# The last unit of a tiled matrix product: a bank of its own for one product, and another queue for two stores

## The chip, the cores and the metric

The kernel runs on one core of one Trainium2 chip. The metric is the device time of one execution in microseconds (us). A core has TensorE (PE, matrix products), VectorE (DVE), ScalarE (ACT), GpSimd (POOL) and SyncE (SP). Each works through its own list of instructions in order. DMA transfers are issued from the lists of SP and ACT here; the issuing instruction takes its place in that list, and the transfer itself is carried out by DMA engines. Matrix products are written into PSUM[...]; VectorE and ScalarE read them there.

## The reference

```
attention: q, k, v of (4, 8, 768, 64); each query sees only the keys that
           have the same nearest centroid (16 per head); softmax; times v
x        = the result as (3072, 512)
h        = x @ w_in            # (3072, 2048)
g        = relu(h) ** 2
out      = g @ w_out           # (3072, 512)
```

The change concerns the last part of the last batch, a piece of `g @ w_out`.

## The kernel before

The kernel first does the attention of all heads, with the rounding of the weights beside it. Then it takes the four batches in the order `FEED`, one after the other (n = 0 to 3). For each it computes `g` in `up` (or `first_up`) and then the product with `w_out` in `Down.run` (or `first_down` for n = 0). Both use a scheme that makes a product of two-by-two blocks from seven block products and a number of sums; in `Down` it is used twice, one level inside the other.

`Down.run` goes through `self.units`. A unit is a pair `(of, j)`: `j` is one of the seven products of the outer level, and `of` says which set of rows it is for. For the last batch there are 14 units, the last being `(1, 3)`. Within one unit the inner level makes seven products. `times` makes each with four matmuls that add up in PSUM. Their results go to two banks, `one` and `two`: `one[:, 0]`, `one[:, 1]`, `one[:, 2]` and `two[:, 0]` to `two[:, 3]`, 128 columns each. The order on TensorE is `one[:, 0]`, `two[:, 0]`, `two[:, 1]`, `two[:, 2]`, `two[:, 3]`, `one[:, 2]`, `one[:, 1]`. So `two[:, 3]` is the fourth product of the bank `two`, and `one[:, 1]` the seventh of the unit.

ScalarE copies `one[:, 0]` to the tile `copied`; behind this copy, in ScalarE's list, `self.store()` issues the stores that are noted in `self.stores`. VectorE puts the seven products together in the generator `combine`, which runs one unit later than the products it uses, in two halves. The first half is three adds on `two` into `r`: one of 256 columns on the first two blocks, one of 128 on the third, one of 256 on the fourth. The second half adds `r` to the result tile `c[...]` (512 columns), and adds `one[:, 1:3]` (256 columns). When a result is complete, `combine` notes it in `self.stores`, and `store` sends it out one unit later as two transfers of 128 KB, by `store_block` (L1104), from ScalarE's list.

For the last unit there is nothing to run behind it, and its combining is a little different. The seventh product goes to a bank of its own, `last`. `one[:, 2]` and `last` are added apart, 128 columns each, and each half of the result is stored as soon as it is ready: the half with the sixth from SP's list, the other from ScalarE's. After the loop, `list(waiting)` runs this last combining, and `self.store()` then issues what is still noted: the result `(0, 12)` of the unit in front, which was combined while the last unit's products ran.

The order on each engine is that of the program (`manual_schedule`). Banks come from the pool `banks` of six, in rotation, by `bank_tile`. A wait is set where an instruction reads a tile that another engine writes, and it is for the whole of what has been written into that tile's bank so far in program order.

At the very end all engines load a flag (L1263) and branch (L1276) over a general path that other inputs would need. SP then waits for all transfers to be complete, and the engines meet in a closing barrier (L1460).

Of the kernel before, what the change touches and what calls it, by code (L numbers as in the profile page):

```python
# [18 lines left out]
P = 128  # L19
# [6 lines left out]
def kernel(  # L26
# [10 lines left out]
    nc = tc.nc  # L37

    B, H, S, D = q.shape
# [510 lines left out]
    def sub(out, a, b, eng=nc.vector):  # L550
        return eng.tensor_tensor(out=out, in0=a, in1=b, op=ALU.subtract)  # L551
# [61 lines left out]
    for p in range(NG):  # L613
# [37 lines left out]
        first, last = total[p][:, :, 0:QA], total[p][:, :, QA:S]  # L651
# [71 lines left out]
    def bank_tile(width):  # L723
        return banks.tile([P, width], F32, name="bank", tag="bank")
# [8 lines left out]
    def combine(c, product, width, early=(), behind_copy=None, behind_add=None):  # L733
        (c11, c12), (c21, c22) = c
        waiting = {}

        def bank_of(j):
            if j in waiting:
                return waiting[j]
            bank = bank_tile(width)  # L740
            product(j, bank)
            return bank

        def add(j, *results):
            bank = bank_of(j)
            for out, to in results:
                nc.vector.tensor_tensor(out=out, in0=bank, in1=to, op=ALU.add)  # L747
            if behind_add:
                behind_add(j)

        bank = bank_tile(width)
        product(1, bank)
        nc.scalar.copy(out=c11, in_=bank)
        if behind_copy:
            behind_copy()
        for j in early:
            waiting[j] = bank_of(j)
        add(6, (c12, c11))
        add(2, (c11, c11))
        add(7, (c21, c12))  # L760
        add(5, (c22, c21), (c12, c12))
        sub(c21, c21, bank_of(4))
        add(3, (c12, c12))
# [91 lines left out]
    def plus(out, one, two):  # L855
        nc.vector.tensor_tensor(out=out, in0=one, in1=two, op=ALU.add)
# [42 lines left out]
    def right(j):  # L899
        return {1: w_q[0][0], 2: w_q[1][0], 3: w_q[1][1], 4: w_t.get(4), 5: w_t.get(1),  # L900
                6: w_t.get(2), 7: w_t.get(3)}[j]
# [16 lines left out]
    def slot(k):  # L918
        first = F2 * PAIR + (k % 2) * F4 * P
        return home[k // 2 * 2][:, first : first + F4 * P].rearrange("p (f n) -> p f n", f=F4)  # L920

    def quarters(y):
        return [[y[:, F4 * g : F4 * (g + 1), P * m : P * (m + 1)] for m in range(2)] for g in range(2)]
# [12 lines left out]
    def load_right(j):  # L936
        for k in (1, 2, 0, 3):
            nc.sync.dma_start(slot(k), w_far[j - 1, k].rearrange("p (f n) -> p f n", f=F4))
# [15 lines left out]
    def first_level(g, f):  # L954
        a = block_of(g, f, TWO)
        s1, s2 = (s_home(i)[:, f] for i in range(2))
        plus(s1, a[1][0], a[1][1])
        sub(s2, s1, a[0][0])
        sub(a[1][0], a[0][0], a[1][0])

    def store_third(g, n, f):
        nc.sync.dma_start(g_far[n][f, :, 1:3], g[:, F2 + f, :, THIRD])
        if n % 2 == 0:
            nc.sync.dma_start(g_far[n][f, :, 0], g[:, f, 0, THIRD])
# [12 lines left out]
    def times(bank, left, rhs):  # L977
        for f in range(F4):
            nc.tensor.matmul(  # L979
                bank, lhsT=left[:, f], rhs=rhs[:, f], start=(f == 0), stop=(f == F4 - 1)  # L980
            )
# [6 lines left out]
    class Down:  # L988
# [77 lines left out]
                c[12] = tile(outp, "osb")  # L1066


        def combine(self, of, j, one, two, copied, last=None):
            c = self.c[of]  # L1070
            r = c[{1: 11, 4: 21, 5: 12, 7: 22}[j]] if j in (1, 4, 5, 7) else four_r
            plus(r[:, 0:2], two[:, 0:2], copied.unsqueeze(1).to_broadcast([P, 2, P]))
            plus(r[:, 2], two[:, 2], r[:, 1])
            plus(r[:, 1:4:2], two[:, 3].unsqueeze(1).to_broadcast([P, 2, P]), r[:, 1:3])
            yield
            if j in (2, 3):
                to = c[{2: 11, 3: 12}[j]]
                plus(to, to, r)
                if last is None:
                    plus(to[:, 1:3], one[:, 1:3], to[:, 1:3])  # L1080
                else:
                    plus(to[:, 2], one[:, 2], to[:, 2])
                    self.store_block(of, 12, 1, nc.sync)
                    plus(to[:, 1], last, to[:, 1])
                    self.store_block(of, 12, 0, nc.scalar)
                    return
            else:
                plus(r[:, 1:3], one[:, 1:3], r[:, 1:3])
            if j == 7:
                sub(c[21], c[22], c[21])  # L1090
            elif j == 6:
                plus(r, c[11], r)
                for to in (21, 12):
                    plus(c[to], c[to], r)
                plus(c[22], c[22], c[12])
            for to in {6: (21, 22), 2: (11,), 3: (12,)}.get(j, ()):
                self.stores.append((of, to))
# [8 lines left out]
                self.c[of][to][:, 2 * i : 2 * i + 2],  # L1106
            )

        def store(self):
            for of, to in self.stores:  # L1110
                for i in range(2):
                    self.store_block(of, to, i, nc.scalar)
            self.stores = []

        def run(self):
            first_level(self.g, F2 - 1)
            store_third(self.g, self.n, F2 - 1)
            waiting = None
            for u, (of, j) in enumerate(self.units):
                x, s = self.ahead  # L1120
                y = quarters(right(j))
                copied = spare_tile[:, 4 + u % 2]
                one, two = (
                    bank_tile(4 * P).rearrange("p (i n) -> p i n", i=4) for _ in range(2)
                )
                times(one[:, 0], x[0][0], y[0][0])
                nc.scalar.copy(out=copied, in_=one[:, 0])  # L1127
                self.store()
                times(two[:, 0], x[0][1], y[1][0])
                times(two[:, 1], s[:, 1], slot(1))  # L1130
                times(two[:, 2], x[1][0], slot(2))
                times(two[:, 3], s[:, 0], slot(0))
                times(one[:, 2], x[1][1], slot(3))
                if waiting:
                    next(waiting)
                sub(x[0][1], x[0][1], s[:, 1])
                last = None
                if self.n == B - 1 and u + 1 == len(self.units):
                    last = bank_tile(P)
                times(one[:, 1] if last is None else last, x[0][1], y[1][1])  # L1140
                if u + 1 < len(self.units):
                    if (k := self.units[u + 1][1]) != j:
                        load_right(k)
                    if of and j in LATER:
                        self.load_left(LATER[j])
                    if self.units[u - 1] == (0, 5):
                        sub(self.s1, self.a[0][1], self.s2)
                    self.parts()
                if u == 0:
                    store = third_sums(self.g, self.n, F2 - 1)  # L1150
                    self.find_results()
                    if self.n % 2:
                        self.load_left(4)
                        self.load_left(1)
                    store()
                    if self.n % 2:
                        self.load_left(5)
                if waiting:
                    next(waiting, None)
                waiting = self.combine(of, j, one, two, copied, last)  # L1160
                to_end = len(self.units) - 1 - u
                for kk in LOADS[self.n % 2].get(u, ()):
                    load_x(self.n + 1, kk)
                if to_end == 2 - self.n % 2:
                    sum_x(self.n + 1, 1)
                elif to_end == 0:
                    sum_x(self.n + 1, 2)
            list(waiting)
            sum_x(self.n + 1, 1)
            self.store()  # L1170
# [71 lines left out]
    def load_x(n, kk):  # L1242
        if n < B:
            b = FEED[n]
            if b not in xT:
                xT[b] = xp.tile([P, KT, S], F32, name="xT", tag="x1")
            nc.sync.dma_start(xT[b][:, kk], x_far[b][:, kk])
# [3 lines left out]
    def sum_x(n, steps):  # L1251
        if n < B:
            if n not in x_summed:
                x_summed[n] = [x_sums(FEED[n])]
            for _ in range(steps):
                x_summed[n].append(next(x_summed[n][0]))
# [208 lines left out]
```

## Time and profile before

| What | Value |
|---|---|
| time, median of 3 runs | 886.84 us (885.61 to 886.95) |
| profiled execution, its own time | 885.83 us |
| its span, first to last instruction | 884.0 us (884.04 in the trace's own record) |
| granted TensorE clock, mean | 0.998 |
| PE busy | 876.0 us, 99% of the span |
| DVE busy | 702.7 us, 79% |
| ACT busy | 390.2 us, 44% |
| from 872.00 to 878.40 us: PE, DVE, ACT busy | 5.48, 4.04, 0.27 us |
| from 878.40 us to the end: PE, DVE, ACT busy | 0, 0, 0 us |
| DMA share from 878.40 us to the end | 0.32 |

The profile is of one execution; its time is 1.8 us longer than the span, and the instructions lie in the span. A span of an engine's list that isn't counted as busy (issue of DMAs, branches, waits) can still be read: such rows have the engine's name with a q, as ACTq. The page's chain of waits is empty for this trace. In the timeline a row with x8 for PE is one product of four matmuls, each recorded twice.

### The profile page before, as it was taken

The numbers are of one execution on the slowest core, as the hardware profiler recorded it, in microseconds if no ns is written. First come the engines' busy times: TensorE is split into PE (matmuls) and PEld (weight loads), VectorE is DVE, ScalarE is ACT, GpSimd is POOL, SyncE is SP. The second block draws the span as 40 slices with busy tenths as digits, with TensorE's granted clock in tenths as the row PEclk, the third lists the DMA queues.
The fourth block names the chain that finished last, engine by engine and source line by source line (L and its number), as shares of the span: only waits on it lengthen the run. The fifth ranks groups of instructions, "written<-read, shape, count | busy, mean of one in ns | idle before, by whom it ended". The sixth has DMA issues, their size and how long they took to land.

```text
span 884.0 us, 14579 instructions
## 1 busy us (share of the span) xinstructions
PE 876.0 (99%) x5379; PEld 584.3 (66%) x5379; DVE 702.7 (79%) x1272; ACT 390.2 (44%) x621; POOL 145.5 (16%) x168
## 2 busy tenths in 40 slices
PE   9999999999999999999999999999999999999997
PEld 5444444444444455568855589996557975569996
DVE  6799888888888999999756586796568786576785
ACT  5877667777666657740045510003543024530000
POOL 0000000000010247730132200013320042300000
PEclk9999999999999999999999999999999999999999
DMA  6777787767763335236811156583113751118563
GB/s 251 177 189 193 218 263 186 201 179 211 212 161 101 102 134 171 72 121 225 309 36 49 42 166 194 155 268 105 51 51 105 237 162 37 52 60 247 153 196 115
DMA packets 166401, 136.04 MB, mean 154 GB/s; under 512 B 58826, under 2 KB 140082, under 8 KB 166066
## 3 DMA queue, kind: packets, MB, share of 16 engines
q1 hardware_dynamic: 149650, 119.65, 45.3%
q10 hardware_dynamic: 16672, 15.37, 5.7%
q8 instruction: 45, 0.74, 0.3%
q14 instruction: 34, 0.28, 0.1%
HBM read 82.10 MB, written 41.89 MB: 140 GB/s over the span
## 4 chain that ended last, share of the span: by engine, by line


## 5 line engine op out<-in xcount | busy, mean ns | idle before, releaser
L457 ACT ACTIVATE ex<-sc 128x1024 f32<-128x1024 f32 x144 | 144.3, 1026 | 37.5 <-PE sc L441 32.5
L747 DVE TENSOR_TENSOR g<-bank,g 128x384 f32<-128x384 f32 x192 | 102.5, 552 | 73.2 <-PE bank L790 67.8
L441 PE MATMUL sc<-qkT 64*128 64x512 f32 (+1 forms) x768 | 150.5, 484 | 0.0
L766 ACT ACTIVATE g<-g 128x384 f32<-128x384 f32 x122 | 63.4, 520 | 104.4 <-DVE g L747 100.2
L441 PEld LDWEIGHTS sc<-qkT 64*128 64x128 f32 x768 | 65.7, 188 | 42.1 <-issue 30.2
L790 PE MATMUL bank<-xT,w_in 128*128 128x384 f32 x256 | 93.2, 487 | 0.0
L790 PE MATMUL bank<-xT,w_s 128*128 128x384 f32 x256 | 93.1, 486 | 0.0
L1127 ACT COPY spare<-bank 128x128 f32<-128x128 f32 x35 | 9.3, 264 | 189.9 <-PE bank L979 165.9
L790 PE MATMUL bank<-x_t,w_s 128*128 128x384 f32 x256 | 93.0, 486 | 0.0
L475 PE MATMUL av_a<-ex,v_raw 128*64 128x512 f32 x384 | 85.9, 596 | 0.0
L460 DVE TENSOR_TENSOR total<-total,ex 128x1024 f32<-128x1024 f32 x64 | 78.7, 1229 | 6.5
L571 POOL TENSOR_TENSOR w_s<-w_in 128x256 f32<-128x256 f32 x32 | 25.2, 787 | 315.9 <-PE bank L979 148.4
L979 PE MATMUL bank<-home,l 128*128 128x128 f32 x560 | 74.0, 275 | 0.0
L790 PEld LDWEIGHTS bank<-xT,w_s 128*128 128x128 f32 x256 | 48.6, 190 | 34.2 <-issue 0.6
L790 PEld LDWEIGHTS bank<-x_t,w_s 128*128 128x128 f32 x256 | 48.6, 190 | 33.9
L790 PEld LDWEIGHTS bank<-xT,w_in 128*128 128x128 f32 x256 | 48.3, 190 | 33.7 <-DVE g L551 0.6
L161 POOL TENSOR_TENSOR w_in<-w_in,w_raw 128x512 int32<-128x512 int32 x16 | 21.4, 1337 | 294.3 <-DVE w_in L153 294.3
L979 PEld LDWEIGHTS bank<-home,l 128*128 128x128 f32 x560 | 68.2, 192 | 0.1
L767 ACT ACTIVATE g<-g 128x384 f32<-128x384 f32 x122 | 63.8, 523 | 3.9
L475 PEld LDWEIGHTS av_a<-ex,v_raw 128*64 128x64 f32 x384 | 26.1, 137 | 51.0 <-issue 50.3
L450 PE MATMUL sc<-rows 64*128 64x512 bf16 (+1 forms) x360 | 58.8, 323 | 0.0
L790 PE MATMUL bank<-x_t,w_in 128*128 128x384 f32 x128 | 46.5, 486 | 0.0
(192 smaller groups left out, 1408.6 us busy)
## 6 DMA issues: line engine op xcount, KB each, us to landing
home<-w_far SPq DMA_DIRECT2D x92, 256.0 KB
words<-flat SPq DMA_DIRECT2D x26, 384.0 KB
w_raw<-in_moe_w_in_dram SPq DMA_DIRECT2D x16, 512.0 KB
w_raw<-in_moe_w_out_dram SPq DMA_DIRECT2D x16, 512.0 KB
w_far<-home SPq DMA_DIRECT2D x28, 256.0 KB
g<-g_far SPq DMA_DIRECT2D x28, 256.0 KB
v_raw<-in_v_dram SPq DMA_DIRECT2D x16, 384.0 KB
g_far<-third SPq DMA_DIRECT2D x24, 256.0 KB
```

The source lines that it names most:

```text
L161: nc.gpsimd.tensor_tensor(out=dst, in0=dst, in1=lo, op=ALU.add)
L441: nc.tensor.matmul(sc[i][:, e, cols], lhsT=qkT[pair][rows, NCH + c], rhs=qkT[pair][rows, n.start // P : n.stop // P], start=first, stop=no ...
L450: nc.tensor.matmul(sc[i][:, e, cols], lhsT=ohT[pair][rows, 1, c * P : (c + 1) * P], rhs=ohT[pair][rows, 0, columns(i)], start=first, stop= ...
L457: nc.scalar.activation(out=ex[i], in_=sc.pop(i), func=ACT.Exp, scale=SCALE)
L460: eng.tensor_tensor(out=out, in0=a, in1=b, op=ALU.add)
L475: nc.tensor.matmul(bank[D * e : D * (e + 1), 0 : n.stop - n.start], lhsT=raw_v[pair][:, e, c], rhs=ex[i][:, e, cols], start=c == 0, stop=c ...
L571: nc.gpsimd.tensor_tensor(out=s1, in0=a[1][0], in1=a[1][1], op=ALU.add)
L747: nc.vector.tensor_tensor(out=out, in0=bank, in1=to, op=ALU.add)
L766: nc.scalar.activation(out=to, in_=to, func=ACT.Relu)
L767: nc.scalar.square(to, to)
L790: nc.tensor.matmul(bank, lhsT=operands[j][0][:, kk], rhs=operands[j][1][:, kk], start=(kk == 0), stop=(kk == H2 - 1),)
L979: nc.tensor.matmul(bank, lhsT=left[:, f], rhs=rhs[:, f], start=(f == 0), stop=(f == F4 - 1))
```

## The change

In the last unit of the last batch, the block product that was `two[:, 3]` is written to a new bank `five` (128 columns). `combine` reads `five` in its third add. In all other units `five` is `two[:, 3]`, as before. The bank `last` is taken at the unit's start with `five`.

The result `(0, 12)`, two transfers of 128 KB, is issued from SP's list instead of ScalarE's, and before the last combining in program order. So SP's list ends with these two stores and the store of the last result's first half; ScalarE's list ends with one store, that of the other half, where it ended with three.

```diff
-        def combine(self, of, j, one, two, copied, last=None):
+        def combine(self, of, j, one, two, five, copied, last):
...
-            plus(r[:, 1:4:2], two[:, 3].unsqueeze(1).to_broadcast([P, 2, P]), r[:, 1:3])
+            plus(r[:, 1:4:2], five.unsqueeze(1).to_broadcast([P, 2, P]), r[:, 1:3])
...
-        def store(self):
+        def store(self, queue=nc.scalar):
             for of, to in self.stores:
                 for i in range(2):
-                    self.store_block(of, to, i, nc.scalar)
+                    self.store_block(of, to, i, queue)
...
+                ends = self.n == B - 1 and u + 1 == len(self.units)
+                five = bank_tile(P) if ends else two[:, 3]
+                last = bank_tile(P) if ends else None
...
-                times(two[:, 3], s[:, 0], slot(0))
+                times(five, s[:, 0], slot(0))
...
-                last = None
-                if self.n == B - 1 and u + 1 == len(self.units):
-                    last = bank_tile(P)
-                times(one[:, 1] if last is None else last, x[0][1], y[1][1])
+                times(last if ends else one[:, 1], x[0][1], y[1][1])
...
-                waiting = self.combine(of, j, one, two, copied, last)
+                waiting = self.combine(of, j, one, two, five, copied, last)
...
+            if self.n == B - 1:
+                self.store(nc.sync)
             list(waiting)
             sum_x(self.n + 1, 1)
             self.store()
```

## The prediction

> **What bounds the kernel now.** The page's first part says that TensorE is never free:
>
> ```profile
> PE 876.0 (99%) x5379; PEld 584.3 (66%) x5379; DVE 702.7 (79%) x1272; ACT 390.2 (44%) x621; POOL 145.5 (16%) x168
> ```
>
> The change takes no matmul away and adds none, so it can only act where TensorE is done: behind the last product. The chain of waits on the page is empty for this trace, so I followed the end by hand. First the timeline of the last 10 us (start, length, engine, line, operation):
>
> ```profile
> 874.38 0.42 DVE L856 TENSOR_TENSOR c<-bank,c 128x256 f32<-128x256 f32 x1
> 874.64 1.06 PE L979 MATMUL bank<-home,l 128*128 128x128 f32 x8
> ...
> 875.53 1.06 PE L979 MATMUL bank<-home,g 128*128 128x128 f32 x8
> 875.80 1.21 DVE L856 TENSOR_TENSOR spare<-bank,spare 128x256 f32<-128x256 f32 x3 [1.00 <-PE bank L979]
> ...
> 876.42 1.06 PE L979 MATMUL bank<-w_out,g 128*128 128x128 f32 x8
> 877.04 0.69 DVE L856 TENSOR_TENSOR c<-c,spare 128x512 f32<-128x512 f32 x1
> 877.84 0.49 DVE L856 TENSOR_TENSOR c<-bank,c 128x128 f32<-128x128 f32 x2
> 878.16 0.34 SPq L1104 DMA_DIRECT2D out_dram<-c  x1
> ```
>
> See the 1.00 us in which VectorE waits: it starts its first add 0.27 us after `one[:, 2]`, the product behind `two[:, 3]`, has started (875.80 against 875.53), so it waited for `two[:, 3]`, though that add reads only `two[:, 0:2]`. Then come two more adds on `two`, one of 512 columns and two of 128. The last ends at 878.33, 0.75 us later than TensorE alone would ask: a seventh product started at 876.42, with the usual 0.89 us from one product to the next and 0.27 to the release, is ready at 877.58.
>
> Behind that stands the stores' queue. The timeline from 876 on ends with
>
> ```profile
> 878.36 1.35 ACTq L1104 DMA_DIRECT2D out_dram<-c  x3
> ```
>
> that is, ScalarE issues the last store and, after it, the two of the result in front, which VectorE had finished at 874.80. What follows is in the answers for the lines of the closing branch and the flag's load (count: shortest/median/longest ns, first and last start):
>
> ```profile
> L1263 ACTq TENSOR_LOAD <-flag x1: 572/572/572, 879.7 to 879.7; - x1
> L1276 SPq EVENT_SEMAPHORE  x8: 17/17/17, 881.7 to 882.3; - x8
> L1276 DVEq COMPARE_BRANCH  x1: 72/72/72, 878.5 to 878.5; - x1
> L1276 SPq COMPARE_BRANCH  x1: 58/58/58, 878.5 to 878.5; - x1
> L1276 ACTq COMPARE_BRANCH  x1: 54/54/54, 880.4 to 880.4; - x1
> L1276 DVEq EVENT_SEMAPHORE  x1: 21/21/21, 881.9 to 881.9; - x1
> L1276 ACTq EVENT_SEMAPHORE  x1: 17/17/17, 883.2 to 883.2; - x1
> ```
>
> Each engine loads the flag, branches over the general path, and needs 2.8 us (ACT) to 3.4 us (DVE) until its next instruction. ACT gets there last, at 883.2. The list of SP's waits shows the meeting:
>
> ```profile
> SPq L1460 <- ACTq L1276: 0.4, 1, 0.4
> ```
>
> SP is through its own waits at 882.8 and waits 0.4 us for ACT; 0.83 us later the span ends at 884.04. So **ACT's order of issue sets the end, with SP only 0.4 us behind**. The transfers do not: the narrow DMA views show the last data at 881.3, before SP's first completion wait at 881.7.
>
> [...]packets of the instruction queues, 0.3 to 0.4 us long, start about 1.0 us after ACT's branch (881.3) and 1.5 us after those of SP and DVE (two at 880.0, amid the stores), and each engine resumes about 1.45 us after such a packet's end. Which packet is whose, I take from this spacing. [...]here the third ACT store took 2.1 us from issue (879.2) to its last packet, the queueing included.
>
> **The change part by part.**
>
> *`two[:, 3]` in its own bank* (`five`). TensorE: same seven products, same order, 0; in the order of instructions no other wait appears than that for the rotating banks, whose former owners, two units back, VectorE had finished by 870.5. VectorE's first add now waits for `two[:, 2]` only, behind which the next product starts at 874.64: 874.64 + 0.27 = 874.91 (VectorE is free at 874.80). The second follows 0.46 us later. The third reads `five`: 875.53 + 0.27 = 875.80, against 876.59 before, 0.79 earlier. Fourth add 0.45 us on, 876.25; fifth 0.80 on (it reads `one[:, 2]`, released at 876.42 + 0.27 = 876.69, covered), 877.05 to 877.34. The sixth, which reads `last`, could start 0.21 us on, at 877.26, but that seventh product is only ready at 877.58: **a new wait of 0.32 us**. It ends at 877.86 instead of 878.33: 0.47 gained. The third add now waits for two engines; if that costs an instruction of its own, the 0.11 us gaps before waiting adds bound it, and the 0.32 us hide it.
>
> *The two stores moved to SP.* ACT loses two issues: 1.35 / 3 = 0.45 each, 0.90. ACT's only store starts at 877.89 and ends at 878.34, so its flag load starts at 878.34, not 879.71: 1.37 earlier, of which 0.47 is the adds and 0.90 the issues. SP gains two issues of 0.34 us at 874.83, when the result is ready. They pass nothing on SP except the store of the last result's half, which comes at 877.37 now; SP waits in front of it for 13.8 us before, so the 0.68 us are hidden by an idle engine. If that cover were gone they would cost at most 0.68. Nobody else waits for SP there.
>
> *The half result on SP* starts 0.79 us earlier (877.37), so SP's branch, its jump and its eight completion waits move by 0.79: ready at 882.0 instead of 882.8.
>
> *Transfers.* The last store's data: 877.89 + 2.1 = 880.0 at the latest, before SP's first wait (881.7 − 0.79 = 880.9, or 880.4 with a quicker fetch). Hidden, by 0.4 us at least.
>
> *Sum.* ACT arrives at 883.2 − 1.37 = 881.8, SP at 882.0. What is late next is SP, so the end moves by 883.2 − 882.0 = 1.2 us. [...]The trace can't show how the fetches fall among two stores instead of four; bounds are 0.5 us less (SP delayed once more by as much) and 0.5 us more. I take **1.3 us**. The profiled execution (885.83, of which 884.04 is the span) would go to 884.5. It stands 1.0 below the median 886.84 of runs that spread from 885.61 to 886.95; on the median's scale the forecast is 886.84 − 1.3 = **885.5**.
>
> **The rivals.** The bound for telling a change from none is 0.2%, 1.8 us here; my forecast lies below it.
>
> *Faster than it* (885.0 or less). Only one store is issued on ACT, perhaps in 0.34 us instead of 0.45 (the rows show 338 to 505 ns): 0.11. With fewer packets about, ACT's and SP's jumps could be 0.3 us shorter: 1.37 + 0.11 + 0.3 = 1.8, so 885.0. For it: SP's and DVE's fetch was late by 0.5 amid the stores. Against: ACT's jump, which decides, ran when the stores had nearly drained. The spread of the runs, 1.3 us, adds to this case.
>
> *Nearly nothing.* Something else holds the end: SP's jump is delayed another 0.5 us because its fetch now falls on the two last stores, 882.5 against 883.2, a gain of 0.7: 886.1. Or the adds don't start early, because the wait is still for the whole of it. Then 0.47 and SP's 0.79 go: ACT at 882.3, SP at 882.8: 0.4 saved, 886.4. Against this, the order of waits puts a TensorE wait on the third add now.
>
> *Slower.* [...]If the jump needs a second fetch in line (1.0 to the packet, 0.4 for it, 1.45 to resume: 2.8 us more), ACT arrives at 881.8 + 2.8 = 884.6 instead of 883.2: +1.4, 888.2. It decides from 1.4 us of extra jump. Nothing speaks for it: the four jumps seen range only from 2.8 to about 4.
>
> **How the numbers follow.** The likeliest case, 1.0 to 1.6 us gained, gets 0.50; nearly nothing 0.12; both lie within 0.2%, with the mild slower ones. Faster by over 0.2% gets 0.34 with the runs' spread; the slower case 0.04 over the bound. So within: 0.62. The range goes from 884.4 (1.8 gained and half the runs' spread) to 886.8 (no gain); about 0.8 lies inside.
>
> **What would show it.** Right: VectorE's idle 1.00 us before the first add shrinks to about 0.1, and a wait of some 0.3 us for TensorE appears before the last add, which ends about 877.9; SP issues three stores from 874.8 on, ACT one at 877.9; ACT's flag load starts about 878.3 and SP no longer waits for ACT; the span is 882.6 to 882.9. Wrong: the first add still at 875.8; a flag load on ACT later than 878.6; a jump over 3.5 us on ACT or SP; or any shift in the times before 870 us, where the change has nothing to do.

## The result, and the profile after

| | before | after |
|---|---|---|
| median, first comparison (8 runs each) | 886.81 us | 884.10 us |
| ratio, first comparison | 1 | 0.9973 (95%: 0.9962 to 0.9983) |
| ratio, second comparison (10 runs against 24) | 1 | 0.9982 (95%: 0.9973 to 0.9991) |
| profiled execution, its own time | 885.83 us | 884.70 us |
| its span | 884.0 us | 882.9 us |
| start of the last product on TensorE | 876.42 us | 876.67 us |
| **tail**: from there to the end of the span | 7.62 us | 6.25 us |

The changed kernel is faster, by less than 0.4%. The forecast was 885.5 us, 1.3 us below the median of before. The first comparison gives 2.4 us (0.0027 × 886.8; the medians differ by 2.7), the second 1.6 us; gains of 1.5 to 2.4 us agree with both intervals. The measured median, 884.1, lies 0.3 us below the lower end of the range; the ratio, taken from 886.84, gives 884.4, on that end. The two profiles alone differ by 1.1 us in span: that of after is of the slowest of its eight runs, that of before of a run 1.0 us below its median. TensorE also came to its last product 0.25 us later in the profile of after, and VectorE's adds before 870 us are later by as much, so this comes from before the changed unit. The two profiles of the unchanged kernel further down differ by 0.5 us in the same way. So I count from the start of the last product, and call this time the tail. It fell by 1.4 us.

The timeline of after's last 10 us shows the same steps as that of before:

```profile
874.63 0.42 DVE L856 TENSOR_TENSOR c<-bank,c 128x256 f32<-128x256 f32 x1
...
874.88 1.06 PE L979 MATMUL bank<-home,l 128*128 128x128 f32 x8
875.08 2.84 SPq L1104 DMA_DIRECT2D out_dram<-c  x3
875.15 1.28 DVE L856 TENSOR_TENSOR spare<-bank,spare 128x256 f32<-128x256 f32 x3
...
876.47 0.69 DVE L856 TENSOR_TENSOR c<-c,spare 128x512 f32<-128x512 f32 x1
...
876.67 1.06 PE L979 MATMUL bank<-w_out,g 128*128 128x128 f32 x8
877.27 0.29 DVE L856 TENSOR_TENSOR c<-bank,c 128x128 f32<-128x128 f32 x1
877.77 0.29 DVE L856 TENSOR_TENSOR c<-bank,c 128x128 f32<-128x128 f32 x1 [0.21 <-PE bank L979]
```

See that VectorE's wait of 1.00 us before the three adds is gone; that SP issues three stores from 875.08 on; and that the last add now waits 0.21 us for TensorE, which it didn't before. The stores' rows, by tile (count: shortest/median/longest ns, first and last start), and the rows of the closing branch and of ScalarE's flag load:

```profile
L1104 ACTq DMA_DIRECT2D out_dram<-c x3: 338/339/444, 872.5 to 878.1; - x3
L1104 SPq DMA_DIRECT2D out_dram<-c x3: 333/338/769, 875.1 to 877.6; - x3
```

```profile
L1279 SPq EVENT_SEMAPHORE  x8: 17/17/17, 880.6 to 881.2; - x8
L1279 SPq COMPARE_BRANCH  x1: 58/58/58, 878.0 to 878.0; - x1
L1279 ACTq COMPARE_BRANCH  x1: 54/54/54, 879.0 to 879.0; - x1
L1279 ACTq EVENT_SEMAPHORE  x1: 17/17/17, 882.0 to 882.0; - x1
```

```profile
L1266 ACTq TENSOR_LOAD <-flag x1: 477/477/477, 878.5 to 878.5; - x1
```

ScalarE's list now has one store left, started at 878.1; its flag load comes at 878.5 and it resumes behind the branch at 882.0. It is still the last to arrive, as SP's waits say:

```profile
SPq L1463 <- ACTq L1279: 0.4, 1, 0.4
```

### The profile page after: what moved, and what is told of

Same layout as the page of the kernel before. It is cut to its first block, busy times and chain, and to the rows that moved or that the text cites. A ratio compares the mean times of both kernels' runs of the same rounds, so it can differ in the third digit from the quotient of the medians.

```text
span 882.9 us, 14581 instructions
## 1 busy us (share of the span) xinstructions
PE 876.2 (99%) x5379; PEld 584.6 (66%) x5379; DVE 703.4 (80%) x1272; ACT 390.0 (44%) x621; POOL 145.8 (17%) x168
## 4 chain that ended last, share of the span: by engine, by line
PE 99%; DMA 0%; ACT 0%; DVE 0%; issue 0%
PE bank L790 33%; PE bank L979 25%; PE sc L441 14%; PE av_a L475 10%; PE bank L871 5%; PE av_b L475 5%; PE sc L450 4%; PE sc L329 1%; PE sc L494 1%; DMA q_raw<-in_q_dram 0%; PE av_a L289 0%; ACT ex L457 0%; PE av_a L274 0%; PE sc L274 0%; PE av_b L274 0%; PE av_b L289 0%
```

## The experiments

Theory A is that of the prediction: the end comes when the last engine is over its branch, ScalarE first of all, so that what counts is how early the last instruction in front of the branch is issued. Rival B: the stores in flight lengthen the fetches of the code behind the branch, or the wait for completion, and the gain comes from fewer stores there. Rival C: the excess over 1.4 us is scatter from earlier stages. Rival D: the relief of ScalarE's list counts, and not the place in the order. All ratios are to the kernel before; tails come from one profile each. A fetch stands for the packets of the instruction queues (q8 and q14) that run between an engine's branch and its next instruction; that they bring the code behind the branch is read from their place and not said by the records. A jump is the time from the start of an engine's branch to its next instruction; where it is given to 0.01 us, it is from the trace's own records, as the tails are.

| run | tail, us | ratio (95%) |
|---|---|---|
| before, again | 8.3 | 1.0005 (0.9996 to 1.0013) |
| own bank only | 7.8 | 0.9996 (0.9988 to 1.0005) |
| stores moved only | 7.4 | 0.9992 (0.9984 to 1.0000) |
| both, but stores from ScalarE | 6.2 | 0.9979 (0.9969 to 0.9989) |
| after, again | 6.1 | 0.9982 (0.9973 to 0.9991) |
| both, but stores behind the last combining | 8.2 | 0.9994 (0.9986 to 1.0002) |
| before, no branch | 5.6 | 0.9978 (0.9963 to 0.9993) |
| after, no branch | 4.1 | 0.9956 (0.9943 to 0.9970) |
| before, thin stores | 7.6 | 0.9992 (0.9983 to 1.0000) |
| after, ScalarE held up | 7.3 | 0.9991 (0.9983 to 1.0000) |
| after, flag loaded early | 6.8 | 0.9980 (0.9973 to 0.9986) |
| the same, half result from ScalarE | 5.8 | 0.9974 (0.9967 to 0.9981) |

**The two kernels again.** No edit.

> The kernel before, unchanged, for a second profile. Tail is used here for the time from the start of the last product on TensorE to the end of the span: 7.62 us in the first profile of before, 6.23 in that of after. Theory A (the order of issue on ScalarE, and its jump over the general path, set the end): ratio 1.000, tail 7.4 to 7.9 again, ScalarE's next instruction after its branch 6.8 us after the last product's start. Rival B (the stores that are in flight delay the fetch of the code behind the branch by a changing amount, and the first profile caught a short one): the tail differs by 0.5 us or more from the first, up to 9. Rival C (what the measured ratio shows beyond 1.4 us is scatter of the stages before the last unit): tail 7.6, and the start of the last product moves by 0.5 us or more between the profiles.

> The changed kernel, for a second profile and ratio. Theory A: tail 6.1 to 6.4, ratio 0.9985 (1.4 us of 886.8). Rival B: tail 6.2 with little spread while that of before is wide; ratio 0.9973 again. Rival C: tail 6.2, ratio anywhere from 0.997 to 0.9995.

The tail of after came back within 0.2 us. That of before didn't: 8.34 us instead of 7.62. The rows of the closing branch in this second profile of before, and SP's waits:

```profile
L1276 SPq EVENT_SEMAPHORE  x8: 17/17/17, 881.2 to 882.9; - x8
...
L1276 ACTq COMPARE_BRANCH  x1: 54/54/54, 879.9 to 879.9; - x1
...
L1276 ACTq EVENT_SEMAPHORE  x1: 17/17/17, 883.1 to 883.1; - x1
```

```profile
SPq L1276 <- SPq L1276: 4.3, 2, 3.1
SPq L1460 <- PEq L1460: 0.6, 2, 0.5
```

SP's eight completion waits now take 1.7 us (881.2 to 882.9) where they took 0.6, and SP no longer waits for ScalarE: the wait for a store's completion set this end. But it is the smaller part of the 0.72 us that this tail is longer. ScalarE branched 3.97 us after the last product's start in both profiles, and its jump took 3.22 us instead of 2.76, so it arrived 0.45 us later. In the first profile the span ended 0.89 us after ScalarE had arrived. With ScalarE as the last, this span would have ended at 884.0 (an estimate: 883.11 + 0.89); it ended at 884.27, so the late completion added 0.27 us.

The DMA view from 881.65 to 882.40 us of that profile shows what was late:

```profile
DMA packets 11, 0.02 MB, mean 33 GB/s; under 512 B 1, under 2 KB 9, under 8 KB 9
...
q10 hardware_dynamic: 9, 0.01, 6.2%
```

Nine packets of ScalarE's queue, a sixteenth of a store's 144, so one DMA engine's share, run from 881.68 to 882.35, after 0.7 us in which hardly any of a store's data moved (the view from 880.90 to 881.65 has one packet of it, of 0.00 MB). A 16 KB instruction packet (queue q8) ran from 879.96 for 1.73 us, to 881.69, and the nine begin at 881.68. That it sat in their way on one engine is what the times suggest; the records don't name the engine. In the first profile of before a packet of that size ran from 880.75 to 882.15, and the stores' last packets moved beside it, until 881.38. So rival B may have a part in this second, later end; the first profile doesn't show it. Of C, the part about the tail fell; but the start of the last product does move by 0.5 us between the two profiles of before (876.42, 875.93), and by up to 2.4 us over all runs.

**Each half alone.**

```diff
 own bank only:      -            if self.n == B - 1:
                     -                self.store(nc.sync)
 stores moved only:  -                five = bank_tile(P) if ends else two[:, 3]
                     +                five = two[:, 3]
```

> Only the bank of its own for the fourth product of bank two; the three stores on ScalarE stay. Theory A: the last add ends 0.47 us earlier against the last product, everything on ScalarE moves with it: tail 7.15, ratio 0.9995. Rival B: four stores are still in flight together, so the fetches are delayed as before: tail 7.1 to 7.6 and scattered, ratio 0.9995 to 1.000. If the bank were the main part of the measured gain, the ratio would be 0.998 or less.

> Only the two stores of the result in front moved to SyncE, ahead of the last combining; the product stays in bank two. Theory A: ScalarE's flag load 0.90 us earlier against the last product, SyncE's last store where it was; SyncE decides, tail 7.2, or 6.7 if its fetch comes 0.5 us sooner: ratio 0.9990 to 0.9995. Rival B: with two stores in flight and not four the fetches run free: tail 6.2 to 6.7, ratio 0.997 to 0.998, nearly all of the gain.

Neither half brings a gain that its interval sets apart from none; the middles are 0.35 and 0.7 us, and the whole change has 1.6 to 2.4. The unchanged kernel itself came out 0.4 us the other way, so the smaller middle says nothing. In the first, SP is ready but ScalarE, with three stores to issue, is 1.8 us behind it:

```profile
SPq L1461 <- ACTq L1277: 1.8, 1, 1.8
```

Its tail, 7.8, is longer than the 7.15 expected, as ScalarE's jump took 3.4 us (880.5 to 883.9). In the second, ScalarE arrives at 882.9 and SP is over its completion waits only at 883.1, with no wait for ScalarE left:

```profile
L1279 SPq EVENT_SEMAPHORE  x8: 17/17/17, 882.5 to 883.1; - x8
...
L1279 ACTq EVENT_SEMAPHORE  x1: 17/17/17, 882.9 to 882.9; - x1
```

The tail of 7.4 is near theory A's 7.2, with SP deciding. Rival B's 6.2 to 6.7 didn't come: with the two stores gone from the end, SP's jump still took 3.3 us, where it took 3.2 in the kernel before. In the run with the own bank alone, all three stores left on ScalarE, it took 2.6. So the number of stores at the end doesn't by itself set it. In the kernel before, two engines arrive within half a microsecond of each other; to shorten one uncovers the other. The own bank moves both, the stores' move only ScalarE.

**Queue or place.**

```diff
 ahead, from ScalarE:   -                self.store(nc.sync)
                        +                self.store(nc.scalar)
 behind, from SP:       -            if self.n == B - 1:
                        -                self.store(nc.sync)
                         list(waiting)
                         sum_x(self.n + 1, 1)
                        -            self.store()
                        +            self.store(nc.sync if self.n == B - 1 else nc.scalar)
```

> As the changed kernel, but the two stores are issued ahead of the last combining from ScalarE, not SyncE. Theory A and rival B: place in the order counts and not the queue; ScalarE is idle when the result is ready: tail 6.2, ratio as the change, 0.997 to 0.9985. Rival D (it is the relief of ScalarE's list that counts): two more issues of 0.45 us on ScalarE, tail 7.1, ratio 0.9995.

> As the changed kernel, but the two stores are issued from SyncE behind the last combining in program order, so behind the store of the last result's half. Theory A: ScalarE's list is as in the changed kernel, but SyncE issues two more stores of 0.34 us before its branch: SyncE arrives 0.7 us later than in the changed kernel and decides: tail 6.6 to 6.9, ratio 0.999. Rival B: four stores in flight again amid the fetches: tail 7.3 or more, ratio 0.9995 or above. Rival D (only ScalarE's list counts): tail 6.2.

The place counts. From ScalarE but ahead of the last combining, the tail is 6.2 and the ratio that of the change; rival D falls. In this profile SP was the last to arrive and not ScalarE: their jumps took 3.0 and 2.7 us. From SP but behind the last combining, the interval reaches beyond no gain; its middle is 0.5 us, and theory A's 0.999 lies in it. The tail, 8.2, is longer than theory A allowed (6.6 to 6.9), but this profile is of the slowest of the kernel's 13 runs, 1.3 us above their median, so 8.2 isn't its usual tail. Both jumps were the longest that these engines have in any profile, 3.7 us on SP and 3.9 on ScalarE:

```profile
SPq L1277 <- SPq L1277: 3.7, 1, 3.7
```

```profile
L1277 ACTq COMPARE_BRANCH  x1: 54/54/54, 879.6 to 879.6; - x1
...
L1277 ACTq EVENT_SEMAPHORE  x1: 17/17/17, 883.5 to 883.5; - x1
```

Four stores had been issued just ahead of the two branches (879.6 and 879.8), three by SP from 878.2 to 879.8 and one by ScalarE, which had issued it by 879.0. This one profile is as rival B has it; the run's times fit theory A too.

**Without the branch.** The load of the flag, `tc.If` and the general path are removed from both kernels.

> The kernel before without the load of the flag, the branch and the general path behind it (left out; other inputs would need them). Theory A: no jump of 2.8 to 3.4 us per engine; what is left is ScalarE's last issue, 3.3 us after the last product's start, the last data 2.1 us behind it, then the waits and the barrier of some 1.7 us: tail 6.0 to 7.0, ratio 0.998 to 0.999. If the data's completion rather than the jump had set the end: tail as before, 7.6, ratio 1.000.

> The changed kernel without the flag's load, the branch and the general path. Now the last store's completion sets the end: issue at 1.2 us after the last product's start against 2.8 for the last of the three in the kernel before. Theory A: tail 1.3 to 1.6 us shorter than that of the kernel before without the branch. Rival B (the gain is in the fetches): with no branch no code has to be fetched, and the two differ by 0.5 us or less in the tail.

The tails fall by 2.0 and 2.2 us, so the jump is on the path in both. That of before, 5.6, is below the 6.0 to 7.0 expected: ScalarE's last issue had ended at 879.1, 3.3 us after the last product's start, and SP was through its waits and in the barrier at 880.6, 1.5 us later. The two still differ by 1.5 us, where B alone allowed 0.5; the ratios lie 2.0 us apart, with intervals that overlap. The profiles of these two runs count 72 and 71 packets of instructions; those of before and after count 79 each, eight of them in the tail. If the rest is as it was, at most one is left in the tails here (an estimate: 72 − (79 − 8)), and the gain is there all the same: the last issue comes earlier, and what follows it, jump or completion, starts earlier. SP's waits without the branch, in the kernel before and in the changed one, are

```profile
SPq L1455 <- DMA out_dram<-c: 2.5, 4, 1.4
```

```profile
SPq L1458 <- DMA out_dram<-c: 1.7, 2, 1.3
```

that is, the stores' completion. In the first profile of before the jump covered it: the last packet ended at 881.38 and SP's first wait came at 881.73.

**Fewer bytes in the same lists.** `store_block` takes a number of rows, 16 for the last four stores of the kernel before.

> The kernel before with its last four stores cut to 16 of 128 partitions (the other rows are left out): the same list on ScalarE and SyncE, an eighth of the bytes in flight. Theory A (ScalarE's list and a jump of fixed length set the end): ScalarE's next instruction after its branch 6.8 to 7.2 us after the last product's start as in the two profiles of before, tail 7.6, ratio 0.9995 to 1.000. Rival B (the stores in flight lengthen the jumps): jumps of SyncE and ScalarE fall from 3.1 and 2.8 to 3.2 us to 2.6 us or less, completion no longer decides: tail 7.1 or less, ratio 0.999 or below; if it is all of the gain, tail 6.2.

SP's jump fell from 3.2 to 2.6 us, but the end stayed with ScalarE, whose jump took 2.9, and the tail at 7.6:

```profile
SPq L1460 <- ACTq L1276: 1.0, 1, 1.0
```

So in the kernel before transfers do seem to lengthen SP's way, by about 0.6 us in one profile, but they are not what the change shortens at ScalarE. The ratio's middle, 0.7 us, would fit the loss of late completions and of longer jumps as in the second profile of before; its interval reaches 1.0000, so this isn't shown.

**ScalarE held up.** Four copies of 128 columns behind its last store.

```diff
             list(waiting)
+            if self.n == B - 1:
+                for _ in range(4):
+                    nc.scalar.copy(out=copied, in_=spare_tile[:, 0])
```

> The changed kernel with four copies of 128 columns put behind ScalarE's last store (work added that computes nothing). Theory A: ScalarE's branch comes about 1.1 us later (4 times 0.27), and as it was already the last to arrive, the end moves by as much: tail 7.0 to 7.3 instead of 6.2, ratio to the kernel before 0.999 to 1.000. Rival B (transfers and fetches in flight decide, or SyncE's completion waits): tail 6.2 to 6.5.

```profile
L1282 ACTq EVENT_SEMAPHORE  x1: 17/17/17, 882.2 to 882.2; - x1
```

```profile
SPq L1466 <- ACTq L1282: 1.5, 1, 1.5
```

ScalarE resumes 6.5 us after the last product's start (882.2 against 875.72) where it was 5.4 in after, 1.1 later; the tail grew by 1.1; SP waits 1.5 us for it. This is the plainest sign that ScalarE's arrival sets the end here, and, with SP's waits of 0.4 and 0.3 us for it, the end of the changed kernel in its two profiles.

**Two further steps.** The flag's load is moved to the start of the second batch for all engines; then the last result's first half is stored from ScalarE too.

```diff
-            again = nc.values_load(flag[0:1, 0:1], min_val=0, max_val=1)   # left to the end of the lists
+            again = nc.values_load(flag[0:1, 0:1], min_val=0, max_val=1)   # below manual_schedule, ahead of n = 1
...
-                    self.store_block(of, 12, 1, nc.sync)
+                    self.store_block(of, 12, 1, nc.scalar)                 # second step only
```

> The changed kernel with the load of the flag moved on all engines to the start of the second batch, so that nothing but the branch stands behind ScalarE's last store. Theory A: ScalarE arrives 0.5 to 0.6 us earlier; SyncE, 0.3 to 0.4 us behind it, decides then: tail 5.8, against 6.2, if the load costs nothing in the middle; on TensorE's list there it may cost up to 0.5 us, which would take the gain back. Ratio 0.9975 to 0.9985. Rival B: tail as the changed kernel, 6.2.

> As the run with the early flag, and the last result's first half is stored from ScalarE as well, where 0.34 us fit between the two adds; SyncE's list then ends with the two stores of the result in front. Theory A: SyncE branches 1.7 us earlier and is left with waiting for the last completion; ScalarE arrives 4.6 to 4.9 us after the last product's start: tail 5.4 to 5.8, ratio 0.997 to 0.998. If the last store's completion decides instead, 2.1 us after an issue 1.2 us behind the last product, with 0.6 us of waits and 1.3 of barrier: tail 5.2. Rival B: tail 6.0 or more.

With the early load ScalarE resumes 4.9 us after the last product's start, 0.5 earlier; but SP's jump took 3.3 us in this profile and it decides: tail 6.8, ratio no better than the change. With the second step SP branches at 876.2 and is through at 880.1, ScalarE is last again, and the tail is 5.8, the shortest with the branch in place. Its ratio, 0.9974, is below that of the early load alone by 0.5 us, and the intervals overlap; that it beats the changed kernel is likely by the tail and not shown by the times.

## Why the prediction was right, and where its size was off

- **The view from which it started held.** TensorE's 99% told that only what lies behind the last product could change.
- **The own bank** did what was worked out. Against the start of the last product the first add came at −1.52 us (expected 874.91 − 876.42 = −1.51), and the last ended at +1.39 (expected +1.44). The new wait for the last product is there, 0.21 us instead of 0.32.
- **The moved stores** left ScalarE's list as expected: its last store at +1.4 (expected +1.47), the flag load at +1.8 (expected +1.92), the arrival at +5.4 (expected +5.4). SP's issues were hidden, though one took 0.77 us and not 0.34.
- **That the arrival agrees so well is in part luck.** ScalarE's branch came 1.63 us earlier against the last product (+3.97 to +2.34), more than the 1.37 expected, because the adds, the store's issue and the flag load were each a little shorter. Its jump took 0.26 us longer (2.76 to 3.02), which gave the surplus back.
- **What is late next** was wrong. I had SP arrive last, at +5.6, and one of my signs was that SP would no longer wait for ScalarE. It does: SP's jump took 2.65 us instead of 3.19, so SP was ready 0.4 us before ScalarE, which stayed the last. So the end moved with ScalarE, for which the sum had 1.37, and not by SP's 1.2; the tail fell by 1.4 between the first two profiles. The order isn't fixed: with the stores issued ahead from ScalarE, SP was last, at nearly the same tail.
- **The step that was mis-sized** is the sum's base: one profile of before, taken as its usual end. The sum left transfers out on both sides, because SP's first wait came behind the last data, and it kept ScalarE's jump at the length of that one profile. It read the instruction packets as 0.3 to 0.4 us long; in the same profile one of 16 KB ran from 880.75 for 1.41 us, while the last stores' data moved. A second profile of before had a tail of 8.3, 0.45 us of it from a longer jump and 0.27 from late completion, so the change takes away 1.4 us against the one and 2.1 to 2.2 against the other. A mean between them would agree with both comparisons. How often each case comes isn't known from two profiles, so that this explains the surplus is likely and not shown. The "faster" rival had put its surplus into shorter jumps and a shorter issue. The issue was shorter by the 0.11 us it named. ScalarE's jump was 0.3 us longer than in the first profile of before and 0.2 to 0.3 shorter than in the second; its part stays open.
- **The range** was meant to take in half the spread of the runs below a gain of 1.8; the medians differed by 2.7. The second comparison came back at 1.6. The slower rival didn't show: the longest jump was 3.9 us, in a kernel that isn't the changed one. One sign of being wrong, a shift in the times before 870 us, did come, 0.24 us; the unchanged kernel's two profiles are shifted by more, so it doesn't speak of the change.
- **Still open**: what moves the start of the last product from run to run (875.7 to 878.1 in the profiles, the lists up to there being the same in all but the early-flag kernels and those without the branch), and whose fetch each instruction packet is, which I take from spacing only.

## What to carry to other kernels

Behind the last product, read each engine's list down to the barrier: a store that is ready early but stands behind one that is late costs its issue there (0.45 us each in the kernel before), and a flag load (0.57 us) and a jump (2.8 us on ScalarE) wait behind that. When two engines arrive within half a microsecond, as SP and ScalarE did here (0.4 us), shorten both or expect little: each half alone gave 0.35 and 0.7 us here in the middle of intervals that reach to none, both together 1.6 to 2.4. Take a second profile of the kernel before when the tail is what you predict; one of two had another end.

## What the runs showed of the hardware that was not expected

From a branch to the next instruction, ScalarE and SP took between 2.6 and 3.9 us. In the first profiles of before and after, packets of instructions ran in between: within ScalarE's jump four started in that of before (880.75 to 882.74) and five in that of after (879.45 to 881.95). The longest jumps, 3.7 and 3.9 us, came in a profile where four stores had been issued just ahead of the branches; but with as many stores ScalarE's took 2.8 to 3.4 in three others, so the stores alone don't set the length. SP's was 2.6 with an eighth of the bytes, and also with the own bank and the whole bytes.

That instruction packets hold up data in turn is not shown. In the second profile of before, nine packets of a store began at 881.68, where a 16 KB instruction packet ended at 881.69, and SP's completion waits went on to 882.9. In the first, the last stores' packets moved until 881.38 beside a packet of that size that ran to 882.15.
